# A linear-attention layer with a squared-ReLU feed-forward layer: where the per-token sums are kept, how the weights are laid out and loaded, and the order of the steps

## The chip, the cores and the metric

The kernel runs on one core of one Trainium2 chip. The metric is device time in microseconds (us) of one execution, the median of several runs. The engines in this text are TensorE (PE: matmuls; PEld: its weight loads), VectorE (DVE), ScalarE (ACT), GpSimd (POOL) and the queue of SyncE (SP), which issues most DMA transfers.

## The reference, cut to what matters

The first stage is a linear attention with a decaying state, for 4 batches and 8 heads of 768 tokens with 48 channels. The second is a feed-forward layer with weights of 384 x 2048 and 2048 x 384.

```python
def _attn_ref(r, k, v, w, u):
    state = zeros((B, H, D, D))
    for t in range(S):
        cur = einsum('bhd,bhe->bhde', u[None] * kt, vt)
        y[:, :, t] = einsum('bhd,bhde->bhe', rt, state + cur)
        state = w[None, :, :, None] * state + einsum('bhd,bhe->bhde', kt, vt)
    return y
def _moe_ref(x, w_in, w_out):
    r = np.maximum(x @ w_in, 0.0)
    return (r * r) @ w_out
```

All inputs and the output are float32. The output has 3072 x 384 elements.

## The kernel before, in words

The work is cut into 24 units: 6 chunks of 128 tokens, and in each chunk the 4 batches; unit i belongs to chunk i // 4. Each unit goes through these steps, and each step is a small function that emits a few instructions:

- load (L263): r, k and v of the unit, 192 KB each, by SP's queue, in runs of 48 floats.
- scale (L286, DVE): r and k times powers of the decay, to bf16, into one of NPAD padded buffers (rkw). cast_v (L290, ACT) makes vb from v.
- Turning r and k (rkT): for the first NPE = 7 units PE transposes them (turn, L306) and ACT evicts the result (L310); the later units use a DMA transpose on SP's queue (turn_dma, L295).
- at (L323, PE): products of tokens within the chunk, into two PSUM banks; mask (L335, DVE) multiplies them by a triangle and writes am.
- rk (L315, DVE) multiplies the turned r and k; diag (L341, PE) sums it with u for each token and head, into the last 8 columns of the bank of y; diag_v (L349, DVE) makes dv, those sums times v.
- state_mm (L357, PE) forms what the chunk adds to the state, in a bank of its own; state_add, state_decay (L369 to L375, DVE) and state_cast (L381, ACT) bring the state to the next chunk.
- y_mm (L389 and L395, PE): am times vb, and from the second chunk on turned r times the state, added up in the bank of y. Its first matmul does not clear the bank, since diag has begun it. evict_y (L404, DVE) adds dv.
- x: the first NPY = 6 units are turned by PE (L420) and evicted by ACT (L424), the later ones by a DMA transpose (L413).
- mm1 (L436, PE): four steps a unit, each of 12 matmuls with 128 x 128 weights from w_in_sb; relu (L444, ACT), square (L453 on DVE or L451 on ACT, in turn).
- mm2 (L460, PE): four steps a unit of 4 matmuls with 384 columns of w_out; evict_o (L467) and store (L497). The last unit's mm2 is done in two halves (L475, L486, L488, L493).

The weights come by GpSimd's queue (weights, L273 and L277), which also turns float32 into bf16: w_in and w_out each in four pieces of 384 KB (counted in bf16). Ahead of each piece a one-element copy (gate, L269) holds GpSimd until k of a given unit has landed. The order is the list `front` (L523): U is the load of a unit, I and O are the pieces of w_in and w_out, and a piece is gated by the unit named last before it.

The order of everything is planned when the program is built. Plan.run walks through modelled time: each engine takes, of its steps whose inputs are ready and whose buffers or PSUM banks are free, the one with the lowest rank. The step's cost, a lag until its result can be used, and for DMA its queue are given with plan.add (L513 to L658). Ranks are 4 x unit plus an offset: mm1 comes L1 = 9 places and mm2 L2 = 20 places behind the front of its own unit. The engines then execute in this order, each waiting for what it needs. `room` gives the buffers of each kind, and the call of plan.run the banks that each kind may hold of the eight: at 4 (state products among them), y 2, h 4 (mm1's results and turns), o 2.

Of the kernel before, what the change touches and what calls it, by code (L numbers as in the profile page):

```python
# [1 line left out]

# [13 lines left out]
class Plan:  # L16
# [6 lines left out]
    def __init__(self):  # L23
        self.steps = []
        self.at = {}
        self.users = {}
        self.place = {}

    def add(self, key, engine, cost, emit, needs=(), rank=0.0, new=(), uses=(), lag=0.3, move=None):
        s = dict(key=key, engine=engine, cost=cost, emit=emit, rank=rank, new=new, lag=lag, move=move)  # L30
        s["needs"] = [n for n in needs if n is not None]
        self.at[key] = s
        self.steps.append(s)
        for x in tuple(new) + tuple(uses):
            self.users.setdefault(x, []).append(s)

    def run(self, room, banks, count):
# [15 lines left out]
        def done(s):  # L53
            return "ready" in s and s["ready"] <= t + tiny

        def fits(s):
            names = [x[0] for x in s["new"]]
            for name in set(names):
                if name in banks:
                    continue  # L60
                ring, m = rings[name], room[name]
                for n in range(len(ring) - m, len(ring) - m + names.count(name)):
                    if n >= 0 and not all(done(x) for x in self.users[ring[n]]):
                        return False
            wanted = [name for name in names if name in banks]
            if wanted:
                for n, x in held.items():
                    if x is not None and all(done(u) for u in self.users[x]):
                        held[n], since[n] = None, max(u["ready"] for u in self.users[x])
                if sum(x is None for x in held.values()) < len(wanted):  # L70
                    return False
                for name in set(wanted):
                    mine = sum(x is not None and x[0] == name for x in held.values())
                    if mine + wanted.count(name) > banks[name]:
                        return False
            return True

        while left:
            for e, mine in todo.items():
                if free[e] > t + tiny:  # L80
                    continue
                for s in mine:
                    if s["move"] and sum(x[1] for x in queues[e]) > 4.0:
                        continue
                    if all(done(self.at[k]) for k in s["needs"]) and fits(s):
# [11 lines left out]
                        if s["move"]:  # L97
                            queues[e].append([s, s["move"][0], free[e] + 0.9])
                        else:
                            s["ready"] = free[e] + s["lag"]  # L100
# [6 lines left out]
            later += [s["ready"] for s in order[-400:] if s.get("ready", 0.0) > t + tiny]  # L107
# [8 lines left out]
            for x in moving:  # L116
                x[1] -= step * x[0]["move"][1] / whole
                if x[1] <= 1e-7:
                    queues[x[0]["engine"]].pop(0)
                    x[0]["ready"] = t + x[0]["lag"]  # L120
# [4 lines left out]
def kernel(  # L125
# [21 lines left out]
    NPE = 7  # L147
    NPY = 6
    NPAD = 4
    SQUARES = 'MA'  # L150
# [4 lines left out]
    loads = ctx.enter_context(tc.tile_pool(name="loads", bufs=5))  # L155
# [3 lines left out]
    mpool = ctx.enter_context(tc.tile_pool(name="mpool", bufs=5))  # L159
    psum = ctx.enter_context(tc.tile_pool(name="psum", bufs=1, space=PSUM))  # L160
    banks = [psum.tile([128, 512], F32, name=f"bank{n}") for n in range(8)]
    plan = Plan()
# [105 lines left out]
    def weights(i, q, which):  # L268
        nc.gpsimd.tensor_copy(gate, tiles[i]["kt"][:, 0, :1])  # L269
        if which == "I":  # L270
            sl = slice(q * dff // NQ, (q + 1) * dff // NQ)
            src = moe_w_in.rearrange("(ko ki) f -> ki ko f", ki=128)
            nc.gpsimd.dma_start(out=w_in_sb[:, :, sl], in_=src[:, :, sl])  # L273
        else:
            sl = slice(q * NF // NQ, (q + 1) * NF // NQ)
            src = moe_w_out.rearrange("(ko ki) f -> ki ko f", ki=128)
            nc.gpsimd.dma_start(out=w_out_sb[:, sl, :], in_=src[:, sl, :])  # L277
# [59 lines left out]
    def diag(i):  # L337
        t = tiles[i]
        t["y"] = bank("y", i)[:, : dm + H]
        for p in range(HP):  # L340
            nc.tensor.matmul(  # L341
                out=t["y"][:, dm:], lhsT=t["rk"][:, p, :], rhs=uwb[:, p, :],
                start=(p == 0), stop=(p == HP - 1), skip_group_check=True,
            )

    def diag_v(i):
        t = tiles[i]
        t["dv"] = work.tile([C, H, D], F32, name="dv")
        nc.vector.tensor_tensor(  # L349
            t["dv"], t["vb"], t["y"][:, dm:].unsqueeze(2).to_broadcast([C, H, D]), ALU.mult  # L350
        )

    def state_mm(i):
        t = tiles[i]
        t["s"] = bank("at", i, 2)[:, :dm].rearrange("p (a d) -> p a d", a=HP)
        for p in range(HP):
            nc.tensor.matmul(  # L357
                out=t["s"][:, p, :], lhsT=t["rkw"][:, 1, p].rearrange("p o e -> p (o e)"),
                rhs=t["vb"][:, 2 * p : 2 * p + 2, :].rearrange("p h d -> p (h d)"),
                start=True, stop=True, skip_group_check=True,  # L360
            )
# [21 lines left out]
    def y_mm(i):  # L383
        c, b = units[i]
        t = tiles[i]
        y = t["y"][:, :dm].rearrange("p (h d) -> p h d", h=H)
        for o in range(2):
            for p in range(HP):
                nc.tensor.matmul(  # L389
                    out=y[:, 2 * p + o, :], lhsT=t[f"am{o}"][:, p, :], rhs=t["vb"][:, 2 * p + o, :],  # L390
                    start=False, stop=c == 0 and o == 1 and p == HP - 1, skip_group_check=True,
# [9 lines left out]
    def evict_y(i):  # L401
        t = tiles[i]
        t["yb"] = work.tile([C, dm], BF16, name="yb")
        nc.vector.tensor_tensor(t["yb"], t["y"][:, :dm], t["dv"].rearrange("p h d -> p (h d)"), ALU.add)  # L404
# [21 lines left out]
    def mm1(i, m, s):  # L426
# [5 lines left out]
        for a in range(4 // m):  # L432
            f = s * (4 // m) + a
            for n in range(NK):
                turned = w_in_sb[:, n, f * 128 : (f + 1) * 128]
# [66 lines left out]
    L1, L2 = 9, 20  # L502
# [4 lines left out]
    def add(*a, lag=0.2, **kw):  # L507
        plan.add(*a, lag=lag, **kw)

    def copy(*a, **kw):  # L510
        plan.add(*a, lag=1.2, **kw)

    add("w0", ACT, 3.6, None, rank=-1e3)  # L513
    add("log", PE, 0.64, spread_log, rank=-1e3, needs=["w0"], new=[("h", "log")])
    add("w", ACT, 0.5, do(power, wpos, up), rank=-1e3, needs=["log"], uses=[("h", "log")])
    add("wk", ACT, 0.5, do(power, wneg, down), rank=-1e3, needs=["w"], uses=[("h", "log")])
    copy("begin", SP, 0.74, None, rank=-1e3, move=(0.4, 16))
    copy("wu", SP, 0.9, columns, rank=-99.85, move=(0.1, 16))
# [4 lines left out]
    front = ['U0', 'U1', 'I0', 'U2', 'I1', 'U3', 'I2', 'I3', 'U4', 'O0', 'O1', 'O2', 'O3', 'U5']  # L523
    place = {what: -100 + n for n, what in enumerate(front)}
    seen = -1
    for what in front:
        if what[0] == "U":
            seen = int(what[1:])
        else:
            q = int(what[1])  # L530
            copy(
                (what[0], q), POOL, 1.0, do(weights, seen, q, what[0]), rank=place[what], move=(2.05, 74),
                needs=[("kt", seen)], uses=[("ld", seen)],
            )
    for i in range(NU):
# [3 lines left out]
        rank = place.get(f"U{i}", a - 20)  # L539
        for n, name in enumerate(("rt", "kt", "vt")):  # L540
            copy(
                (name, i), SP, 0.45, do(load, i, name), rank=rank + 0.1 * n, move=(1.03, 16),
                new=[("ld", i)] if n == 0 else (), uses=[("ld", i)] if n else (),
            )
        for x in range(2):
# [6 lines left out]
            ("vb", i), ACT, 0.405, do(cast_v, i), rank=a + 0.5, needs=[("vt", i), ("rkT", i) if i < 4 else ("scale", i, 1)],  # L552
# [14 lines left out]
        else:  # L567
            copy(("rkT", i), SP, 0.45, do(turn_dma, i), rank=a - 30, needs=both, move=(1.9, 32), new=[("rkT", i)], uses=[("rkw", i)])
# [6 lines left out]
        elif i - 1 in PAIRED:  # L575
            add(("at", i), PE, 0.0, None, rank=a - 3, needs=[("at", i - 1)], lag=0.0)
# [7 lines left out]
        add(("diag", i), PE, 0.105, do(diag, i), rank=a + 2, needs=[("rk", i), "uwb"], new=[("y", i)], uses=[("rk", i)])  # L584
        add(("dv", i), DVE, 0.465, do(diag_v, i), rank=a + 2, needs=[("diag", i), ("vb", i)], new=[("dv", i)], uses=[("y", i), ("vb", i)])
        if c < NCH - 1:
            add(
                ("s", i), PE, 0.17, do(state_mm, i), rank=a + (5 if c else 8), needs=[("scale", i, 1), ("vb", i), ("at", i)],
                new=[("at", i, 2)], uses=[("rkw", i), ("vb", i)],
            )  # L590
            add(
                ("sadd", i), DVE, 0.68, do(state_add, i), rank=a + (6 if c else 3.2),
                needs=[("s", i), ("stb", before) if c else "wend"], uses=[("at", i, 2)],
            )
            if c > 0:
                add(("sdec", i), DVE, 0.27, do(state_decay, i), rank=a + 4 + 4, needs=[("sadd", i)])
            add(
                ("stb", i), ACT, 0.71, do(state_cast, i), rank=a + 6 + 4,
# [4 lines left out]
            needs=[("mask", i, 0), ("mask", i, 1), ("vb", i), ("diag", i), ("stb", before) if c else None],  # L603
            uses=[("am", i, 0), ("am", i, 1), ("vb", i), ("rkT", i), ("y", i)],
# [8 lines left out]
        else:  # L613
            copy(("xT", i), SP, 0.45, do(x_dma, i), rank=a - 30, needs=xneed, move=(0.7, 32), new=xnew, uses=[("yb", i)] + xuse)
    begun = 0
    step = 0
    for m in GROUPS:
# [3 lines left out]
        for s in range(4 * m):  # L621
            rank = 4 * i + s + L1 + 1 * (m - 1)
            add(
                ("m1", i, s), PE, (0, 0.668, 0.655, 0, 0.647)[m], do(mm1, i, m, s), rank=rank,
                needs=[("xT", i + n) for n in range(m)] + [("I", s // m), None if b == 0 and s == 0 else ("m1", i - b, 0)],
# [9 lines left out]
        for j in range(i, i + m):  # L635
            a = 4 * j
            squares = [[("sq", i, s) for s in range(q * m, q * m + m)] for q in range(NQ)]
            if j < NU - 1:
                for q in range(NQ):
                    add(  # L640
                        ("m2", j, q), PE, 0.652, do(mm2, j, q), rank=a + q + L2 + 1 * (m - 1),
# [4 lines left out]
                copy(("out", j), SP, 0.42, do(store, j), rank=a + 4 + L2, needs=[("osb", j)], move=(0.8, 110), uses=[("osb", j)])  # L646
                continue
            for n in range(2):
# [9 lines left out]
                copy(("out", j, n), SP, 0.42, do(store_half, j, n), rank=a + 4 + L2, needs=[("osb", j, n)], move=(0.45, 110), uses=[("osb", j)])  # L658
    room = dict(
        ld=5, rkw=NPAD, g=2, rkT=4, vb=4, rk=4, am=8, dv=4, yb=4, xT=3, gr=5, osb=5,  # L660
    )
    for s in plan.run(room, dict(at=4, y=2, h=4, o=2), len(banks)):
# [32 lines left out]
```

## Time and profile before

| | |
|---|---|
| median of 3 runs | 180.88 us (180.58 to 181.18) |
| the profiled execution | 180.29 us |
| its span, first to last instruction | 178.5 us |
| mean granted TensorE clock | 0.997 |
| busy: PE, DVE, ACT, POOL | 165.4, 136.5, 126.8, 12.0 us |
| DMA: hardware queue q1, software queue q0 | 74.4% and 11.2% of 16 engines' span |

Matmuls are pipelined, so the mean duration of one (223 ns in mm1) is longer than the distance between two starts. Where the cost of a PE step is wanted, the distance from start to start on the timeline, or the piece in the chain of waits, is the number to read. Slices are 178.5 / 40 = 4.46 us wide.

### The profile page before, as it was taken

The page shows a single profiled execution, that of the slowest core. Times are in us where ns is not written, and L with a number is a line of the kernel's source. Part 1 is how long each engine was busy: PE and PEld are TensorE (multiplying, and loading weights), DVE is VectorE, ACT ScalarE, POOL GpSimd, SP SyncE. Part 2 cuts the span into 40 slices and gives each one's busy share as a digit, 9 for nine tenths or more (in the row PEclk, how much of TensorE's full clock was granted, in tenths as well). Part 3 has the DMA queues.
Part 4 walks back from the last instruction along what each step waited for, and adds up shares of the span by engine and source line. Part 5 has one row for each costly group of instructions (what it writes and reads, how often), then busy time and mean ns, then how long its engine had stood idle before and what let it go on. Part 6 is the DMA issues. An engine that isn't in the chain of part 4 may idle for free. (4 is left out here: it accounts for less than half of the span.)

```text
span 178.5 us, 5489 instructions
## 1 busy us (share of the span) xinstructions
PE 165.4 (93%) x2270; PEld 132.4 (74%) x2270; DVE 136.5 (76%) x291; ACT 126.8 (71%) x256; POOL 12.0 (7%) x38
## 2 busy tenths in 40 slices
PE   2487889999999999999999999999999999999993
PEld 1366889877786868877868787787787788787872
DVE  4498799854997999979979969988988967573300
ACT  4546399998968466977848985976875875597811
POOL 3451253000000000000000000000000000000000
PEclk9999999999999999999999999999999999999998
DMA  4999999999989998998969998799878976414112
GB/s 89 192 179 219 176 214 201 185 188 193 165 164 113 192 167 175 150 222 178 185 114 225 132 209 177 167 156 218 185 140 196 190 163 199 121 24 70 44 44 88
DMA packets 107682, 28.60 MB, mean 160 GB/s; under 512 B 100873, under 2 KB 107658, under 8 KB 107658
## 3 DMA queue, kind: packets, MB, share of 16 engines
q1 hardware_dynamic: 103944, 25.11, 74.4%
q0 software_dynamic: 3712, 3.15, 11.2%
q8 instruction: 17, 0.28, 0.7%
q14 instruction: 7, 0.06, 0.1%
q10 hardware_dynamic: 2, 0.00, 0.0%
HBM read 20.45 MB, written 4.72 MB: 141 GB/s over the span
## 5 line engine op out<-in xcount | busy, mean ns | idle before, releaser
L436 PE MATMUL bank<-xT,w_in_sb 128*128 128x128 bf16 x1152 | 77.1, 223 | 0.6 <-ACT xT L424 0.6
L436 PEld LDWEIGHTS <-w_in_sb 128*128 128x128 bf16 x1152 | 69.4, 100 | 5.1 <-issue 0.7
L444 ACT ACTIVATE gr<-bank 128x512 f32<-128x512 f32 x96 | 55.0, 596 | 24.2 <-PE bank L436 21.8
L460 PE MATMUL bank<-w_out_sb,g 128*128 128x384 bf16 x368 | 67.5, 326 | 0.0
L460 PEld LDWEIGHTS <-g 128*128 128x128 bf16 x368 | 33.5, 98 | 17.8
L453 DVE TENSOR_TENSOR g<-gr 128x512 bf16<-128x512 f32 x48 | 32.9, 687 | 16.6 <-ACT gr L444 16.3
L335 DVE TENSOR_TENSOR am<-bank,smask 128x512 bf16<-128x512 f32 x48 | 31.1, 685 | 6.3 <-PE bank L323 6.0
L451 ACT ACTIVATE g<-gr 128x512 bf16<-128x512 f32 x48 | 30.3, 634 | 0.9
L467 ACT COPY osb<-bank 128x384 f32<-128x384 f32 x23 | 11.0, 477 | 9.3 <-PE bank L460 9.1
L381 ACT CAST stb<-st 64x192 bf16<-64x192 f32 x40 | 13.9, 347 | 3.8 <-DVE st L375 3.4
L286 DVE TENSOR_TENSOR rkw<-rt,wpos 128x384 bf16<-128x384 f32 x24 | 13.3, 552 | 3.7 <-ACT wpos L238 2.6
L404 DVE TENSOR_TENSOR yb<-bank,dv 128x384 bf16<-128x384 f32 x24 | 13.3, 555 | 2.8 <-PE bank L389 1.7
L349 DVE TENSOR_TENSOR dv<-vb,bank 128x384 f32<-128x384 bf16 x24 | 13.1, 546 | 0.5 <-PE bank L395 0.2
L286 DVE TENSOR_TENSOR rkw<-kt,wneg 128x384 bf16<-128x384 f32 x24 | 13.2, 550 | 0.0
L290 ACT CAST vb<-vt 128x384 bf16<-128x384 f32 x24 | 12.3, 511 | 0.1
L323 PE MATMUL bank<-rkT 64*128 64x128 bf16 x192 | 10.2, 229 | 1.8 <-ACT rkT L310 1.8
L371 DVE TENSOR_TENSOR st<-bank,st 64x192 f32<-64x192 f32 x32 | 11.3, 352 | 0.2
L315 DVE TENSOR_TENSOR rk<-rkT 128x512 bf16<-128x512 bf16 x24 | 10.1, 420 | 1.6 <-ACT rkT L310 1.4
L310 ACT COPY rkT<-bank 128x512 bf16<-128x512 bf16 x14 | 8.2, 587 | 4.3 <-PE bank L306 4.0
L389 PEld LDWEIGHTS <-am 128*128 128x128 bf16 x192 | 8.3, 99 | 3.9 <-issue 2.7
L389 PE MATMUL bank<-vb,am 128*128 128x48 bf16 x192 | 9.1, 187 | 1.7 <-DVE dv L349 1.6
L323 PEld LDWEIGHTS <-rkT 64*128 64x128 bf16 x192 | 5.8, 98 | 5.7 <-ACT rkT L310 2.3
(52 smaller groups left out, 88.1 us busy)
## 6 DMA issues: line engine op xcount, KB each, us to landing
rt<-in_r_dram SPq DMA_DIRECT2D x24, 192.0 KB, 4.4
kt<-in_k_dram SPq DMA_DIRECT2D x24, 192.0 KB, 4.0
vt<-in_v_dram SPq DMA_DIRECT2D x24, 192.0 KB, 4.2
out_dram<-osb SPq DMA_DIRECT2D x23, 192.0 KB, 3.1
w_in_sb<-in_moe_w_in_dram POOLq DMA_DIRECT2D x4, 384.0 KB, 6.1
w_out_sb<-in_moe_w_out_dram POOLq DMA_DIRECT2D x4, 384.0 KB, 8.7
xT<-yb SPq DMA_TRANSPOSE x18, 3.5
rkT<-rkw SPq DMA_TRANSPOSE x17, 3.6
```

The lines of the kernel that those rows point to most:

```text
L286: nc.vector.tensor_tensor(t["rkw"][:, x, :, :, :D], pair(src), pair(wx), ALU.mult)
L323: nc.tensor.matmul(out=t["at"][o][:, p, :], lhsT=t["rkT"][sl, 1, p, :], rhs=t["rkT"][sl, 0, p, :], start=True, stop=True,)
L335: nc.vector.tensor_tensor(am, t["at"][o], smask.unsqueeze(1).to_broadcast([C, HP, C]), ALU.mult)
L349: nc.vector.tensor_tensor(t["dv"], t["vb"], t["y"][:, dm:].unsqueeze(2).to_broadcast([C, H, D]), ALU.mult)
L381: nc.scalar.copy(stb[b][sl, :, o * D : (o + 1) * D], st32[b][sl])
L389: nc.tensor.matmul(out=y[:, 2 * p + o, :], lhsT=t[f"am{o}"][:, p, :], rhs=t["vb"][:, 2 * p + o, :], start=False, stop=c == 0 and o == 1 an ...
L404: nc.vector.tensor_tensor(t["yb"], t["y"][:, :dm], t["dv"].rearrange("p h d -> p (h d)"), ALU.add)
L436: nc.tensor.matmul(out=t["h", s][:, a], lhsT=turned, rhs=chunks[c]["xT"][:, n, b : b + m, :], start=(n == 0), stop=(n == NK - 1),)
L444: nc.scalar.activation(t["gr", s], t["h", s], AF.Relu)
L451: nc.scalar.activation(g, x, AF.Square)
L453: nc.vector.tensor_tensor(g, x, x, ALU.mult)
L460: nc.tensor.matmul(out=t["o"], lhsT=chunks[units[i][0]]["g"][:, f, units[i][1], :], rhs=w_out_sb[:, f, :], start=(f == 0), stop=(f == NF - 1),
```

## The change

The diff is one of many small pieces; they fall into six groups.

- Sums in the state's bank: diag and state_mm become one step, sums, which writes the state products and the diagonal sums into one bank (kind s). y_mm gets a bank that it begins itself, and it no longer needs diag. In the last chunk only the diagonal sums are formed.
- w_in is loaded in two pieces instead of four. w_out is still loaded in four, but a partition gets four adjacent rows of a quarter of it. So that the hidden units match, mm1 takes for each block of 128 hidden units every fourth column of w_in (a step of four elements in the weight operand).
- NPE goes from 7 to 5 and NPY from 6 to 4: units 5 and 6 (r and k) and 4 and 5 (x) are turned by DMA instead of PE. NPAD goes from 4 to 5.
- More buffers: loads 5 to 7, relu results and output tiles 5 to 8, banks of kind h 4 to 5. Squares begin on ACT instead of DVE.
- The order: other ranks (L1 from 9 to 7, loads from 20 to 12 places ahead, DMA transposes from 30 to 10, state steps earlier), another `front` list, and the loads of w and u on SP between the first r and the first k instead of after the first k. vb of the first four units waits for the scaled k, no longer for rkT.
- The planner: the time until a result can be used depends on the engines at both ends (five numbers given to Plan), and DMA steps carry their own queue limits and delays.

The core of the diff:

```diff
-    NPE = 7
-    NPY = 6
-    NPAD = 4
-    SQUARES = 'MA'
+    NPE = 5
+    NPY = 4
+    NPAD = 5
+    SQUARES = 'AM'
...
-    plan = Plan()
+    plan = Plan((0.9, 0.0, 0.1, 0.4, 0.12))
...
         if which == "I":
-            sl = slice(q * dff // NQ, (q + 1) * dff // NQ)
+            sl = slice(q * dff // NQ, (q + 2) * dff // NQ)
...
-            src = moe_w_out.rearrange("(ko ki) f -> ki ko f", ki=128)
-            nc.gpsimd.dma_start(out=w_out_sb[:, sl, :], in_=src[:, sl, :])
+            src = moe_w_out.rearrange("(q ki a) d -> ki q a d", q=NQ, a=NF // NQ)
+            nc.gpsimd.dma_start(out=w_out_sb[:, sl, :], in_=src[:, q])
...
+    def sums(i):
+        c, b = units[i]
+        t = tiles[i]
+        t["s"] = bank("s", i)[:, :dm].rearrange("p (a d) -> p a d", a=HP)
+        t["d"] = bank("s", i)[:, dm : dm + H]
         for p in range(HP):
             nc.tensor.matmul(
+                out=t["d"], lhsT=t["rk"][:, p, :], rhs=uwb[:, p, :],
+                start=(p == 0), stop=(p == HP - 1 and c == NCH - 1), skip_group_check=True,
+            )
+        for p in range(HP if c < NCH - 1 else 0):
             nc.tensor.matmul(
                 out=t["s"][:, p, :], lhsT=t["rkw"][:, 1, p].rearrange("p o e -> p (o e)"),
                 rhs=t["vb"][:, 2 * p : 2 * p + 2, :].rearrange("p h d -> p (h d)"),
-                start=True, stop=True, skip_group_check=True,
-            )
+                start=False, stop=(p == HP - 1), skip_group_check=True,
+            )
...
-        y = t["y"][:, :dm].rearrange("p (h d) -> p h d", h=H)
+        t["y"] = bank("y", i)[:, :dm]
+        y = t["y"].rearrange("p (h d) -> p h d", h=H)
...
-                    start=False, stop=c == 0 and o == 1 and p == HP - 1, skip_group_check=True,
+                    start=(o == 0 and p == 0), stop=c == 0 and o == 1 and p == HP - 1, skip_group_check=True,
...
-                turned = w_in_sb[:, n, f * 128 : (f + 1) * 128]
+                turned = w_in_sb[:, n, :].rearrange("p (q f a) -> p q a f", q=NQ, a=NF // NQ)[:, f // 4, f % 4, :]
...
-    L1, L2 = 9, 20
+    L1, L2 = 7, 20
...
-    copy("wu", SP, 0.9, columns, rank=-99.85, move=(0.1, 16))
+    copy("wu", SP, 1.46, columns, rank=-99.95, move=(0.1, 16, 0.67, 0.1))
...
-    front = ['U0', 'U1', 'I0', 'U2', 'I1', 'U3', 'I2', 'I3', 'U4', 'O0', 'O1', 'O2', 'O3', 'U5']
+    front = ['U0', 'U1', 'I0', 'U2', 'I2', 'U3', 'O0', 'O1', 'O2', 'U4', 'O3', 'U5']
...
-        rank = place.get(f"U{i}", a - 20)
+        rank = place.get(f"U{i}", a - 12)
...
-            copy(("rkT", i), SP, 0.45, do(turn_dma, i), rank=a - 30, needs=both, move=(1.9, 32), new=[("rkT", i)], uses=[("rkw", i)])
+            copy(("rkT", i), SP, 1.24, do(turn_dma, i), rank=a - 10, needs=both, move=(1.5, 26, 0.67, 1.0), new=[("rkT", i)], uses=[("rkw", i)])
...
-        ld=5, rkw=NPAD, g=2, rkT=4, vb=4, rk=4, am=8, dv=4, yb=4, xT=3, gr=5, osb=5,
+        ld=7, rkw=NPAD, g=2, rkT=4, vb=4, rk=4, am=8, dv=4, yb=4, xT=3, gr=8, osb=8,
     )
-    for s in plan.run(room, dict(at=4, y=2, h=4, o=2), len(banks)):
+    for s in plan.run(room, dict(at=4, s=2, y=2, h=5, o=2), len(banks)):
```

## The prediction

> **What bounds the kernel now.** I read the page first: busy shares and the row of slices, then the chain that ended last, then the timeline of TensorE (PE), and last GpSimd's and the DMA queues in the first 40 us.
>
> ```profile
> span 178.5 us, 5489 instructions
> PE 165.4 (93%) x2270; PEld 132.4 (74%) x2270; DVE 136.5 (76%) x291; ACT 126.8 (71%) x256; POOL 12.0 (7%) x38
> PE   2487889999999999999999999999999999999993
> DMA  4999999999989998998969998799878976414112
> L436 PE MATMUL bank<-xT,w_in_sb 128*128 128x128 bf16 x1152 | 77.1, 223 | 0.6 <-ACT xT L424 0.6
> ```
>
> PE has 9 tenths from the seventh slice (about 27 us) to the last but one; only the first six show room. So PE's order sets the end, and time is won where PE idles, runs slowly, or has less to do. The chain from 100 us to 175.5 us is PE nearly throughout. Its pieces (start, duration, what) give the price of a step:
>
> ```profile
> 100.29 0.47 DVE dv L349
> 100.77 0.04 issue
> 100.81 0.36 PE bank L389 x8
> 101.17 0.17 PE bank L395 x4
> 101.34 0.17 PE bank L357 x4
> 101.51 2.60 PE bank L460 x16
> 104.11 1.34 PE bank L436 x24
> ...
> 107.50 0.20 PE bank L389 x8
> ```
>
> 24 matmuls of mm1 take 1.34 us, 56 ns each with their weight load; 8 of y_mm take 0.20 us, 25 ns each with theirs. And at 100.29 PE waits for VectorE's (DVE) dv, since y_mm writes the bank from which dv reads the diagonal sums. After 25 us the waits view puts 1.2 us in 5 waits on this pair.
>
> The start is different. TensorE's timeline shows 12 matmuls of mm1 from 16.99 to 18.27 us, 107 ns each: half the later pace, though the granted clock reads full. The pace turns at about 24 us. Up to 25 us PE waits 7.9 us: 3.1 for the first logarithm, 2.5 for turns of r and k (scaling, and the eviction before them), 1.3 for rkT ahead of the decay products, 0.6 for xT, 0.4 on dv. It never waits for w_in. GpSimd's rows show when weights are asked for:
>
> ```profile
> 9.40 0.92 POOL L273 DMA_DIRECT2D w_in_sb<-in_moe_w_in_dram  x1
> 12.01 0.18 POOL L269 COPY gate<-kt 128x1 f32<-128x1 f32 x1 [1.69 <-DMA kt<-in_k_dram]
> 12.46 0.79 POOL L273 DMA_DIRECT2D w_in_sb<-in_moe_w_in_dram  x1 [0.28 <-issue]
> 17.05 0.18 POOL L269 COPY gate<-kt 128x1 f32<-128x1 f32 x1 [3.80 <-DMA kt<-in_k_dram]
> ...
> 18.39 0.78 POOL L273 DMA_DIRECT2D w_in_sb<-in_moe_w_in_dram  x1
> 24.18 0.39 POOL L269 COPY gate<-kt 128x1 f32<-128x1 f32 x1 [5.01 <-DMA kt<-in_k_dram]
> ```
>
> A quarter of w_in lands 5.8 to 8.7 us after its issue, a quarter of w_out 6.5 to 11.5. The DMA engines are full until some 150 us, so bytes early in the queue decide who starts when.
>
> **The change, part by part.**
>
> Fewer PE transposes. NPE goes 7 to 5, NPY 6 to 4: four half-turns of r and k (units 5 and 6) and two x turns (units 4 and 5) leave PE. On the timeline a half-turn starts at 38.53 and the next step at 38.75 (0.22); an x turn at 35.05, the next step at 35.22 (0.17). 4 x 0.22 + 2 x 0.17 = 1.22 us, all after 22 us where PE is dense. One half-turn also came late (m2 from 45.16 takes 0.65, the turn begins at 46.10): 0.29 us more. ScalarE (ACT) loses 4 x 0.59 + 2 x 0.48 us, which is off the path. In exchange SP's queue gets two more transposes of rkT (1.25 us of issue each, 3.6 to landing) and two of xT (1.20 and 3.5). The loads behind them wait some 4.9 us of queue time in all. That lies beside a backlog: mm1 and mm2 of older units follow the front by L1 and L2 places. Uncovered it would cost one stall of 3.6. In DMA time, q1 takes 94.1% of 50 to 110 us; at some 9.4 units (PE's 6.4 us a unit) that is 6.0 us a unit. A unit's three loads are 3,072 of these packets, at 18.3 ns over 16 engines 3.5 us (8,723 packets in 1.5 to 11 us, 104.8%). So transposes and store are at most 2.5, and two units add at most 5. The DMA row falls to 1 to 7 tenths after 150 us, so I cost it at nothing. Together: -1.5 us, ends -1.5 and +3.6.
>
> Sums in the state's bank. The diagonal sums move from y's bank to that of the state's products; y_mm then no longer waits for dv. The matmuls are the same. The waits view gives 1.6 us in six waits over the run, and the timeline's gaps ahead of the six late y_mm after 25 us, less a normal step, come to about 2.2. What is late next is the second mask, which DVE ends 0.47 us before dv ends; only the 0.6 us gap at 100 us is longer than that. The new wait: the diagonal matmuls now also wait for vb and the scaled k, and PE's queue stands behind them. dv needed vb before too, and PE's waits name vb for only 0.3 us. I take -1.6; ends 0 and -2.2.
>
> Strided weights. Each mm1 weight load reads every fourth column. No row of before reads weights with a step. Packed loads fit into 25 ns with their matmul (y_mm above); mm1's pace is 56. So a strided load may take 2.2 times a packed one at no cost, and above that each ns costs 1,152 ns. The load's own recorded duration, 100 ns, is the upper end: (100 - 56) x 1,152 = 51 us. Below nothing is excluded, as the matmul's own 128 columns set the 56. I take 0, nearest to the 25 ns row, and keep 51 as a rival. [...]
>
> Weights in other pieces. A packet of w_in (2 KB read) takes 99.6 ns (803 in 11 to 19 us at 62.5% of 16 engines), one of w_out (1.5 KB) 76.7 (2,076 in 27.5 to 39 us at 86.5%). The line through both has 8 ns that don't grow with the size, so 4 KB and 6 KB runs save about 8 x 768 + 8 x 1,536 ns over 16 engines, 1.2 us of DMA time: an estimate from two contended windows, hidden behind PE's backlog.
>
> The order at the start. The first w_in piece is twice as large. Issued at 9.4, with 0.9 of issue and some 1.1 to the first byte, its 9.6/2 us of transfer at full or at 62.5% share lands it at 16.2 to 19.1, against a first mm1 at 16.99: up to 2.1 late. But with it two steps of each ready unit can run instead of one. The second half waits for kt of unit 2 (12.01) and not of unit 3 (17.05), and w_out for kt of unit 3 and not of unit 4 (24.18), seven us earlier, queued behind w_in: w_out's first quarter comes some 4 us sooner. The load of unit 4 shares the engines with w_out; by then mm1 of four units (16 x 0.67) and mm2 (4 x 2.6) are in stock. On SP, the two small w and u loads move ahead of the first kt, which then is issued 1.4 us later; its scaling ends at 6.54 and PE's turn of it starts at 7.33 only after an eviction, so 0.8 of that is covered. By 25 us PE has done four mm1 steps; I expect one or two more (0.67 each). I take -1.0, ends +2.5 (late half, late kt) and -4 (dense from 18 us on).
>
> Larger buffers, ranks and the planner's lags change the order everywhere. After 25 us PE's waits beyond dv come to 0.5 us, so there is little to win; I cost them at 0, ends -0.5 and +2. The end (last half store, 175.5 to 178.5) stays.
>
> **Sum.** -1.5 - 1.6 - 1.0 = -4.1. The profiled execution took 180.29 (span 178.5 and 1.8 around it): 176.2 on that scale. The median is 0.6 higher: 176.8.
>
> **Rivals.**
> 1. Strided weights are slower than mm1's pace. For: no row shows them, and weight loads record 100 ns. [...] It decides from 56 + 4.1/1.152 = 59.6 ns a load; at 100 it gives 176.8 + 51 = 228. Slower. Chance 0.10.
> 2. The start turns round: the larger first half comes after mm1 is due and the later unit 4 or 5 and its DMA transpose leave PE idle, which then stays at the 107 ns pace. For: DMA full, every early wait is on a tile's data. Price: +2.5 for the start instead of -1.0, +3.6 for one uncovered transpose: 176.8 + 7.1 = 184 at the end, 181.5 to 184 in the main. Chance 0.13.
> 3. The start opens: PE dense and at full pace from 18 us on, -4 instead of -1: 173.8, with all of the y_mm gaps 173.2. Chance 0.12.
> 4. Nothing gained at the start and masks late in dv's place: only the turns count, 179.4; about 0.08 that it ends between 178.8 and 180.3, and 0.07 that it lies within 0.3%.
> The forecast, 174.5 to 178.8, has 0.50.
>
> **Numbers.** About 0.3% (0.54 us) is what a measurement of this kernel can tell from no change. Faster 0.50 + 0.12 + 0.08 = 0.70, same 0.07, slower 0.10 + 0.13 = 0.23. The range leaves out rival 1 and the outer ends of 2 and 3: 173.3 to 183.0.
>
> **What would show it.** Turns: L306 x40 and L420 x12, 19 and 20 DMA transposes. Sums: no wait of y_mm on dv. Strided: 24 mm1 matmuls in the chain still 1.34 us; 1.5 or more proves rival 1. Start: mm1's matmuls reach 56 ns before 24 us, and PE's slices two to six rise; a wait of mm1 on the w_in load speaks for rival 2. I am wrong if PE gets new gaps after 40 us: then the order, which no row of before shows, is what counts.

## The result, and the profile after

The changed kernel takes 188.12 us (median, 187.92 to 188.76) against 181.03 for the kernel before on the same chip: 1.045 times as long (95% interval 1.039 to 1.050; the quotient of the two medians, 1.039, is its lower end). The forecast was 176.8, with 173.3 to 183.0 as the range. The profiled execution took 188.1 us with a span of 186.3. In what follows a ratio is always to the kernel before on the same chip. Some kernels below have scattered executions: the ratios leave disturbed ones out, the medians and the profiles of e1, e5 and e14 do not, so where the two disagree the ratio is the one to compare.

From the page of the changed kernel: the span, the rows of PE and DMA, and mm1's two groups (now L458). Against the page of before, PE's fifth slice (18.6 to 23.3 us) is empty, and 7s and 8s stand in the middle; the DMA row has a hole of 0 and 3 at 37 to 47 us.

```profile
span 186.3 us, 5404 instructions
PE   3484099999999999999799998999989999979992
DMA  3999999903998797869989969999998997892011
L458 PE MATMUL bank<-xT,w_in_sb 128*128 128x128 bf16 x1152 | 73.5, 222 | 7.8 <-DMA w_in_sb<-in_moe_w_in_dram 5.6
L458 PEld LDWEIGHTS <-w_in_sb 128*128 128x128 bf16 x1152 | 69.0, 115 | 10.8 <-DMA w_in_sb<-in_moe_w_in_dram 6.1
```

PE's timeline shows the hole: one matmul of mm1 runs, and the next waits 5.12 us for a load of w_in.

```profile
17.54 0.29 PE L458 MATMUL bank<-xT,w_in_sb 128*128 128x128 bf16 x1 [0.52 <-DMA w_in_sb<-in_moe_w_in_dram]
22.95 4.75 PE L458 MATMUL bank<-xT,w_in_sb 128*128 128x128 bf16 x47 [5.12 <-DMA w_in_sb<-in_moe_w_in_dram]
```

On the timeline of the weight loads (PEld) the first one of mm1 waits for w_in until 17.53 us, as it must. The second one waits until 22.94, when the second half has landed (in the chain of waits its transfer lasts from 12.70 to 22.90), though the columns that it reads lie in the first half. In the kernel before, no such wait is there.

```profile
17.53 0.11 PEld L458 LDWEIGHTS <-w_in_sb 128*128 128x128 bf16 x1 [0.79 <-DMA w_in_sb<-in_moe_w_in_dram]
22.94 1.20 PEld L458 LDWEIGHTS <-w_in_sb 128*128 128x128 bf16 x12 [5.30 <-DMA w_in_sb<-in_moe_w_in_dram]
```

The chain of waits has 24 matmuls of mm1 in the same 1.34 us as before. So the strided weights don't slow mm1 down, and no line of the page has y_mm waiting for dv any more.

```profile
39.44 1.34 PE bank L458 x24
```

SP's timeline shows the hole in the DMA row: after a load of v at 26.49 (7.08 us to issue) the queue stands until the x transpose of unit 4 can go at 42.96, and the loads of the next units stand behind it. Only a part of this comes from the late start: in e1 below, which has no such wait, the queue still stands from 32.1 to 37.9 us.

```profile
26.49 7.08 SPq L288 DMA_DIRECT2D vt<-in_v_dram  x1
42.96 1.30 SPq L435 DMA_TRANSPOSE xT<-yb  x1
44.31 0.57 SPq L288 DMA_DIRECT2D rt<-in_r_dram  x1
```

After 50 us PE waits 3.4 us on DMA transposes. The first two rows are all of its waits on them there (us in total, times, longest); the third is the kernel before, where y_mm's wait for dv is PE's only one after 50 us:

```profile
PE bank L458 <- DMA xT<-yb: 2.1, 3, 1.2
PE bank L348 <- DMA rkT<-rkw: 1.3, 2, 1.1
PE bank L389 <- DVE dv L349: 0.9, 4, 0.4
```

### The profile page after: what moved, and what is told of

The parts are those of the page before. It is cut to its first block, busy times and chain, and to the rows that moved or that the text cites. A ratio compares the mean times of both kernels' runs of the same rounds, so it can differ in the third digit from the quotient of the medians.

```text
span 186.3 us, 5404 instructions
## 1 busy us (share of the span) xinstructions
PE 164.2 (88%) x2248; PEld 129.9 (70%) x2248; DVE 136.9 (73%) x293; ACT 122.1 (66%) x250; POOL 10.4 (6%) x34
## 4 chain that ended last, share of the span: by engine, by line
PE 53%; DMA 28%; DVE 7%; ACT 5%; SPq 3%; issue 1%; POOL 0%; DVEq 0%; ACTq 0%; POOLq 0%
PE bank L482 22%; PE bank L458 22%; DMA rkT<-rkw 9%; DMA xT<-yb 7%; DMA w_in_sb<-in_moe_w_in_dram 5%; DMA kt<-in_k_dram 4%; DMA rt<-in_r_dram 3%; SPq L288 2%; PE bank L348 2%; ACT gr L466 2%; DVE yb L426 1%; PE bank L411 1%; PE bank L497 1%; ACT g L473 1%; DVE am L360 1%
## 5 line engine op out<-in xcount | busy, mean ns | idle before, releaser
L458 PE MATMUL bank<-xT,w_in_sb 128*128 128x128 bf16 x1152 | 73.5, 222 | 7.8 <-DMA w_in_sb<-in_moe_w_in_dram 5.6
L458 PEld LDWEIGHTS <-w_in_sb 128*128 128x128 bf16 x1152 | 69.0, 115 | 10.8 <-DMA w_in_sb<-in_moe_w_in_dram 6.1
L466 ACT ACTIVATE gr<-bank 128x512 f32<-128x512 f32 x96 | 53.2, 593 | 22.9 <-PE bank L458 22.7
L335 ACT COPY rkT<-bank 128x512 bf16<-128x512 bf16 x10 | 5.9, 585 | 4.2 <-PE bank L331 4.1
```

The lines of the kernel that those rows point to most:

```text
L458: nc.tensor.matmul(out=t["h", s][:, a], lhsT=turned, rhs=chunks[c]["xT"][:, n, b : b + m, :], start=(n == 0), stop=(n == NK - 1),)
L466: nc.scalar.activation(t["gr", s], t["h", s], AF.Relu)
```

## Experiments

Three theories at first: A, the wait for the second half; B, the larger packets of the halves starve the loads; C, the new order. All 18 runs:

| run | what | median us | ratio to before (95%) |
|---|---|---|---|
| changed kernel | | 188.1 | 1.045 (1.039 to 1.050) |
| e1 | changed, w_in in two tiles | 183.0 | 1.016 (1.006 to 1.027) |
| e2 | changed, old layout | 184.1 | 1.022 (1.013 to 1.032) |
| e3 | before, new layout | 196.4 | 1.094 (1.084 to 1.105) |
| e4 | before, new layout, four tiles | 181.0 | 1.004 (1.000 to 1.008) |
| e5 | e1, NPE 7 and NPY 6 | 184.7 | none; 180.8 to 185.3 |
| e6 | changed, four tiles, quarters | 184.4 | 1.021 (1.012 to 1.031) |
| e7 | e1, old ranks | 184.2 | 1.023 (1.014 to 1.032) |
| e8 | before, sums alone | 177.4 | 0.985 (0.976 to 0.994) |
| e9 | e1, old planner | 189.7 | 1.051 (1.046 to 1.055) |
| e10 | e8, new planner | 184.2 | 1.010 (1.003 to 1.017) |
| e11 | e8, new layout, four tiles | 177.2 | 0.981 (0.976 to 0.987) |
| e12 | e8, NPE 5 and NPY 4 | 182.4 | 1.008 (1.003 to 1.013) |
| e13 | e10, limit 4.0 | 183.4 | 1.020 (1.009 to 1.032) |
| e14 | e1, limit 4.0 | 188.1 | 1.036 (1.020 to 1.052) |
| e15 | e1, 20 stores left out | 179.0 | 0.996 (0.992 to 1.001) |
| e16 | e5, limit 4.0 | 184.1 | 1.027 (1.015 to 1.038) |
| e17 | e10, transposes planned 2.2 us earlier | 179.2 | 0.995 (0.991 to 1.000) |
| e18 | e1, transposes planned 2.2 us earlier | 184.8 | 1.026 (1.019 to 1.033) |

### The wait for the other half: e1 to e4

e1:

```diff
-    w_in_sb = const.tile([128, NK, dff], BF16)
+    w_in_sb = [const.tile([128, NK, dff // 2], BF16, name=f"w_in_sb{n}") for n in range(2)]
...
-turned = w_in_sb[:, n, :].rearrange("p (q f a) -> p q a f", q=NQ, a=NF // NQ)[:, f // 4, f % 4, :]
+turned = w_in_sb[f // 8][:, n, :].rearrange("p (q f a) -> p q a f", q=2, a=NF // NQ)[:, f // 4 % 2, f % 4, :]
```

> The changed kernel, with w_in in two tiles, one for each half; nothing else differs. Theory A (a wait that was not needed): in the changed kernel the first strided weight load waits for the first half of w_in, but the second one waits for the second half too, though it reads only the first; PE stands still for 5.1 us (17.8 to 22.95), SP's queue then stands for 10.2 us in front of the x transpose of unit 4, the DMA engines idle from 37.5 to 43 us, and the later waits for loads and DMA transposes are the echo of that. By A the 12 first matmuls of mm1 run together from about 17.5 us and the time falls by 5 us or more: 180 to 183.5. Theory B (big packets): a 4 KB packet of w_in takes its turn at the engines against a 192-byte packet of a load, so the loads starve while w_in comes in; kt of unit 3 still lands at about 24 us, and the time falls by less than 2 us: above 186. Theory C (order): the new ranks and the four added DMA transposes make the PE gaps after 40 us by themselves: about 6 us of gaps after 40 us stay, 183 to 186.

e2 (mm1 and w_out take the old two lines again):

```diff
-turned = w_in_sb[:, n, :].rearrange("p (q f a) -> p q a f", q=NQ, a=NF // NQ)[:, f // 4, f % 4, :]
+turned = w_in_sb[:, n, f * 128 : (f + 1) * 128]
```

> The changed kernel with the old layout of the weights alone: packed columns of w_in as weights, w_out rows as before (1.5 KB runs); w_in still in two halves and the new order. Theory A: the wait for the second half goes as with two tiles, the same time as that run within 0.7 us. Theory B: w_in's 4 KB packets stay and w_out's fall to a quarter; within 1 us of the changed kernel, 187 to 189. If strided weight loads cost PE time by themselves, it is faster than the run with two tiles by more than 1 us, and mm1's matmuls are closer than there.

e3 (the same two places of the kernel before, the other way round):

```diff
-turned = w_in_sb[:, n, f * 128 : (f + 1) * 128]
+turned = w_in_sb[:, n, :].rearrange("p (q f a) -> p q a f", q=NQ, a=NF // NQ)[:, f // 4, f % 4, :]
```

> The kernel before with the new layout alone (strided columns as weights, w_out as four adjacent rows), w_in still in four quarters in one tile. Theory A: the second weight load waits for the second quarter also, a later one for the third and fourth; PE stands 1 to 2 us at about 17 us, and the time grows by 0.5 to 3 us: 181.4 to 184. Theories B and C: no change from the wait, 180.4 to 181.6.

e4 (as e3, but a tile for each quarter):

```diff
+    w_in_sb = [const.tile([128, NK, dff // NQ], BF16, name=f"w_in_sb{n}") for n in range(NQ)]
+turned = w_in_sb[f // 4][:, n, :].rearrange("p (f a) -> p a f", a=NF // NQ)[:, f % 4, :]
```

> The kernel before with the new layout as in the run above, but w_in in four tiles, one for each quarter, so that no load of weights can wait for a quarter that it does not read. Theory A: within 0.6 us of the kernel before, 180.4 to 181.6, and below the run above. If the strided load costs PE time, mm1's distance from start to start is above 56 ns and the time grows by 1.15 us for each ns. Theory B: w_out's packets of 6 KB read hold up the loads of units 4 and 5 in 27 to 39 us; slower by 0.5 to 2 us.

With two tiles the wait is gone. PE's timeline of e1 has the 48 first matmuls of mm1 in one piece from 17.72 us, 5.2 us earlier, and the ratio falls from 1.045 to 1.016, some 5 us:

```profile
17.72 4.74 PE L458 MATMUL bank<-xT,w_in_sb 128*128 128x128 bf16 x48 [0.70 <-DMA w_in_sb<-in_moe_w_in_dram]
```

One part of theory A failed: the later waits on DMA transposes are no echo of this wait. The profile of e1, taken of its longest execution (185.05 us), has 6.3 us of them after 50 us, and e2, which hasn't this wait either, 4.2 us in all.

e3 puts the layout alone into the kernel before, and it costs 9.4% (some 16 us), five times the most that theory A expected (3 us). GpSimd's timeline of e3 shows why: the wait also goes the other way. The third and the fourth load of w_in wait for mm1, which by then reads only the first ones, as if its reads and these loads overlapped, and PE then waits 12.0 us for w_in in all:

```profile
24.94 0.78 POOL L273 DMA_DIRECT2D w_in_sb<-in_moe_w_in_dram  x1 [7.64 <-PE bank L436]
...
32.81 0.78 POOL L273 DMA_DIRECT2D w_in_sb<-in_moe_w_in_dram  x1 [6.90 <-PE bank L436]
```

e4 is the same layout with a tile for each quarter: 0.4% above the kernel before, with an interval of 0.0 to 0.8%. So the layout costs nothing that can be told from no change, and the wait for a piece that isn't read is shown. That e2 (packed, no such wait) and e1 (strided) agree within their intervals says the same of the weight loads. How the framework decides on overlap is not shown; that it takes the whole stretch between a stepped slice's or a load's first and last element would give what is seen.

### What else the change costs: e5 to e8

> The changed kernel with w_in in two tiles, and units 5 and 6 (r and k) and 4 and 5 (x) turned by PE again (NPE 7, NPY 6). Theory C1 (the added DMA transposes): with two tiles SP's queue stood from 32.1 to 37.9 us in front of the x transpose of unit 4, with all later loads behind it, the DMA engines ran at 3 tenths there, and PE then waits 6.3 us on DMA transposes and gaps of 0.7 to 1.8 us come at 57, 84, 115, 132 and 161 us. With the turns on PE the queue doesn't stand there: those waits fall to less than 2.5 us, and the time goes from 183.0 to 180.5 to 182, although PE has 1.2 us more to do. Theory C2 (ranks): the waits on DMA transposes stay at 4 us or more, 182.5 to 184.5.

```diff
-    NPE = 5
-    NPY = 4
+    NPE = 7
+    NPY = 6
```

> The changed kernel with w_in in four tiles and four loads, in the order that the kernel before has (second quarter after unit 2, third and fourth after unit 3, w_out after unit 4). Theory B (the halves starve the loads): kt of unit 3 lands at about 17 us instead of 24, and the time falls below that with two tiles (183.0) by 1 us or more. If B is not it, 182 to 184, with the waits on DMA transposes as they were (about 6 us).

```diff
-front = ['U0', 'U1', 'I0', 'U2', 'I2', 'U3', 'O0', 'O1', 'O2', 'U4', 'O3', 'U5']
+front = ['U0', 'U1', 'I0', 'U2', 'I1', 'U3', 'I2', 'I3', 'U4', 'O0', 'O1', 'O2', 'O3', 'U5']
```

> The changed kernel with w_in in two tiles, and the old places of the loads (20 ahead), of the DMA transposes (30 ahead) and of mm1 (L1 9). Theory C2 (ranks: loads too late): PE's waits on DMA transposes fall below 3 us and the time to 180.5 to 182. Theory C1: SP's queue still stands in front of the x transpose of unit 4, 182.5 to 184.5.

```diff
-    L1, L2 = 7, 20
+    L1, L2 = 9, 20
...
-        rank = place.get(f"U{i}", a - 12)
+        rank = place.get(f"U{i}", a - 20)
```

(and rkT and xT at a - 30.)

> The kernel before with the sums in the state's bank alone (its own ranks for the state's steps, layout and loads as before). As predicted for this step: y_mm no longer waits for dv, and the time falls by 1.6 us, between 0 and 2.2: 178.4 to 180.6. Rival: the diagonal sums now wait for vb, and the time stays within 0.5 us or grows.

```diff
-    for s in plan.run(room, dict(at=4, y=2, h=4, o=2), len(banks)):
+    for s in plan.run(room, dict(at=4, s=2, y=2, h=4, o=2), len(banks)):
```

(with sums, diag_v, y_mm and their steps as in the change, and the old ranks of the state's steps.)

e5 is inconclusive: one execution took 180.8 us and three about 185. e6 and e7 miss: in e6 k of unit 3 passes GpSimd's gate at 16.94 us instead of 24.05 in e1, just as B wants, and the time does not fall. So B is real in the queues, but e6 as a whole gains nothing; in exchange its w_out is asked for at 26.95 instead of 24.52 us, and PE waits 1.5 us for it. The ranks alone (e7) are not it either.

e8 is a hit in sign and mechanism: the sums alone gain 1.5%, and the median, 177.4, lies a little below the expected range. The waits view of e8 from 50 us on has no row at all for PE; in the kernel before, y_mm waited there for dv.

### The parts of the order, one at a time: e9 to e12

> The changed kernel with w_in in two tiles and the old planner (its lags and its limit of 4 us of transfers outstanding on SP's queue), all ranks, costs, buffers and transposes as changed. So far two tiles gave 183.0, and none of undoing the transposes, the halves or the ranks alone went below 182 reliably, while the kernel before with the sums alone gave 177.4: 5.6 us lie in the order. Theory C3 (the planner's rules): the new planner lets SP's queue run later and puts a DMA transpose ahead of loads that could go; with the old rules loads go earlier, PE's waits on DMA transposes and data fall below 2.5 us and the time to 177.5 to 180. Rival C4 (the ranks and the added DMA transposes): no change, 182 to 185.

(edit: the class Plan and the lags 0.2 and 1.2 of the kernel before, in e1.)

> The kernel before with the sums in the state's bank and the new planner with its costs, lags and limits, but the old ranks, transposes, buffers, layout and loads. C3: it loses what lies between, 177.4 becomes 180 to 184, with waits of PE on DMA transposes. C4: within 1 us of 177.4.

(edit: the class Plan and the costs, lags and move figures of the change, in e8.)

> The kernel before with the sums in the state's bank and the new layout (strided columns as weights, four adjacent rows of w_out), w_in in four tiles so that no weight load waits for a quarter that it does not read. If the layout costs nothing by itself, as with the sums left alone: within 0.8 us of 177.4, 176.6 to 178.2.

(edit: e4's two lines and w_out's layout, in e8.)

> The kernel before with the sums in the state's bank and NPE 5, NPY 4: four half-turns and two x turns go from PE to DMA transposes. As predicted for this step: -1.2 to -1.5 us, 175.9 to 176.2; C1 and C4 (SP's queue stands in front of a transpose, the loads behind it come late): 178.5 to 182, with waits of PE on DMA transposes and xT.

```diff
-    NPE = 7
-    NPY = 6
+    NPE = 5
+    NPY = 4
```

e11, sums and new layout, beats both kernels: 0.981 of before, which its interval doesn't tell from the sums alone (e8, 0.985). e9 contradicts C3, that the new planner's rules are what costs in the changed kernel: the old planner with the other changes is slower still, 1.051. But e10 and e12 each put one part into the kernel with sums, and each turns 0.985 into more than 1: the new planner +2.5% (by two of e10's four executions, 181.8 and 183.7 us; the others took 184.7 and 184.9), the four half-turns and two x turns by DMA +2.3%.

In e12 the place can be pointed at. The x transpose of unit 4 takes 5.63 us to issue instead of 1.2, in front of later loads. PE then waits for a mask, for a transpose and for rk between 53 and 57 us, 3.2 us in three waits. That the late loads cause these waits is read from the order of the queue; no run separates it. The windows from 54 us on (start and end, length, busy time of PE, PEld, DVE, ACT, POOL, granted clock, DMA share, GB/s; e12, e12, and e8 for comparison) show the rest: with PE busy 3.20 of 6 us, the granted clock drops to 0.69 and 0.74 for two windows, where e8 has 1.00.

```profile
33.58 5.63 SPq L410 DMA_TRANSPOSE xT<-yb  x1
```

```profile
53.51 0.27 PE L386 MATMUL bank<-vb,am 128*128 128x48 bf16 x4 [0.33 <-DVE am L335]
54.82 0.40 PE L323 MATMUL bank<-rkT 64*128 64x128 bf16 x8 [0.86 <-DMA rkT<-rkw]
57.20 0.27 PE L343 MATMUL bank<-uwb,rk 128*128 128x8 bf16 x4 [1.99 <-DVE rk L315]
```

```profile
54.00:60.00 6.00, 3.20 (x39) 3.03 (x40) 5.71 (x14) 1.81 (x4) 0.00 (x0) 0.69 0.91 169
60.00:66.00 6.00, 6.00 (x68) 4.86 (x65) 4.33 (x9) 3.63 (x7) 0.00 (x0) 0.74 0.77 157
54.00:60.00 6.00, 6.00 (x98) 4.67 (x96) 4.71 (x11) 3.41 (x8) 0.00 (x0) 1.00 1.08 211
```

In the windows on both sides (48 to 54 and 66 to 72 us) the granted clock of e12 is 1.00. The two low ones together lack 3.4 us of full clock (6.00 x 0.31 + 6.00 x 0.26), as much as the mean clock of 0.981 lacks over the span of 181.0 us: an estimate from these figures. The clock is a part of the cost, not all of it: the two of the eight executions with a mean clock of 0.997 or more took 180.2 and 181.3 us, the five at 0.981 took 182.0 to 182.9, and the eighth, at 0.987, 184.2.

### Lost lead, or transposes too late: e13 to e18

Theory D: the loads lose their lead at the start and never make it up. Loads issued by 48 us were 30 in the kernel before, 22 in the changed one, 25 in e1, 27 in e10 (counted on SP's timeline), and from 48 to 144 us every kernel up to there issues 41 to 43 more.

> The kernel before with sums and the new planner, with the planner's limit on transfers outstanding on SP's queue at 4.0 instead of 1.5; nothing else differs from the run with sums and the new planner (184.2, 27 loads issued by 48 us, 27 loads ahead of the first transpose). Theory D: 30 loads stand ahead of the first transpose again, 29 to 30 are issued by 48 us, and the time falls to 177 to 180. If the order of the steps as such is the cause, 182 to 185.

> The changed kernel with w_in in two tiles and the limit at 4.0 instead of 1.5. Only 20 loads instead of 18 stand ahead of the first x transpose, since that transpose is unit 4's. Theory D: a part of the lead comes back: 26 to 27 loads by 48 us, 181 to 183. If the limit is all, below 180.

> The changed kernel with w_in in two tiles, NPE 7 and NPY 6, and the limit at 4.0: 27 loads and one store stand ahead of the first transpose. Theory D: 28 or more loads by 48 us and 178 to 181. If the other ranks, the halves of w_in or the buffers cost by themselves: 182 or more.

```diff
-for x in queues[e]) > 1.5:
+for x in queues[e]) > 4.0:
```

> The changed kernel with w_in in two tiles, with the stores of the first 20 units left out (those rows of the output are not written); SP's order and all else stay. Theory D: the supply is what PE waits for after 50 us, and 20 stores less give it some 0.6 to 0.8 us a unit back: PE's waits on DMA transposes fall below 3 us and the time to 178 to 181. If the supply doesn't bind, within 1 us of 183.0.

```diff
+        if i >= 20:
             nc.sync.dma_start(out=out[b * S + c * C : b * S + (c + 1) * C, :], in_=tiles[i]["osb"])
```

The lead came back (29 loads by 48 us in e13, 30 in e16; 27 in e14) and the time did not. D falls as the cause. e15 shows that transfers do bind in e1: with 20 stores less, PE's waits on DMA transposes after 50 us go from 6.3 us (in e1's one profile, of 185.05 us) to 1.3 (in one of 179.09), and the ratio from 1.016 to 0.996. Whether the engines or SP's queue is relieved, it cannot tell.

Theory E came from the distance between the issue of a transpose of rkT and the first product that reads it (SP's timeline against PE's, each unit). Its median is 7.6 us in the kernel before, 7.0 in e8, 6.8 in e11, but 4.9 in the changed kernel, 5.0 in e1 and 4.8 in e10. To landing a transpose takes 3.6 to 4.5 us (the medians of these runs) and up to 6.1. So the new planner issues transposes just in time.

> The kernel before with sums and the new planner, whose delay from the end of a DMA transpose to its use is set from 0.9 to 3.1 us; all else as in the run with sums and the new planner (184.2). Theory E (transposes issued just in time): the distance from issue to use rises to about 7 us, PE's waits on DMA transposes fall below 1 us, and the time to 177 to 179.5. If the distance is not it: 182 or more.

> The changed kernel with w_in in two tiles and the same longer delay for rkT and xT. Theory E: the distance rises from 5.0 to about 7 us and the time falls from 183.0 to 178.5 to 181; what stays above 177.2 is SP's stand in front of the transposes of units 4 to 6. If the loads or the order as such bind: 182 to 185.

```diff
-                return s["end"] + moved
+                return s["end"] + (3.1 if s["key"][0] in ("rkT", "xT") else moved)
```

In e17 the distance is 6.6 us, the wait of PE on rkT (2.8 us in e10) is gone, and 1.010 becomes 0.995. So in that kernel E accounts for 1.5 of the 2.5% that the new planner costs; the rest, against e8's 0.985, lies within the intervals. The median distance alone doesn't settle it, though: it is 7.0 us in e13 too, where PE still waits 1.8 us on rkT, in two waits, and the ratio is 1.020. PE's timeline of e10 shows one such wait; the transpose had been issued at 104.18, 6.0 us before:

```profile
110.21 0.40 PE L348 MATMUL bank<-rkT 64*128 64x128 bf16 x8 [0.81 <-DMA rkT<-rkw]
```

In e18 the same edit raises the distance to 6.7 us and removes every wait on DMA transposes after 50 us, and the ratio is 1.026, not below e1's 1.016. PE waits for DVE instead:

```profile
PE bank L368 <- DVE rk L340: 2.0, 2, 1.3
PE bank L482 <- DVE g L475: 1.8, 4, 0.7
PE bank L411 <- DVE am L360: 0.5, 2, 0.3
```

So E is not enough in the changed kernel. What stays open: 3.5% lie between e1 and e11 (1.016 and 0.981). The planner and the turns by DMA each cost about 2.4% by themselves in the kernel with sums, and in the full change taking back one of them, or the ranks, or the quarters, does not bring it down for certain. Both taken back at once was not tried. One caution goes with all of these runs: a changed rank, cost, limit or turn makes the planner write a new order for the whole kernel, so each run tests the part together with the order that came out of it.

## Why the prediction was wrong, point by point

- **Strided weights.** The step priced how fast a stepped weight load is read, and there it was right: 56 ns from start to start, 24 matmuls in 1.34 us, rival 1 (228 us) is out, and the time of e4 agrees with the row of y_mm from which it was argued. It failed in not asking what a stepped slice waits for. "It never waits for w_in" was true of before, and the sum went on as if it held after the change, but for a first half that lands up to 2.1 us late. The wait of 5.12 us and its sequel make up about 5 of the 7 to 8 us by which the changed kernel is slower (1.045 against 1.016 in e1). The recorded load grows from 98 to 113 ns (medians of the kernel before and of the changed one) at that same pace.
- **Sums in the state's bank.** Right: -1.6 predicted, -1.5% or 2.8 us by e8's ratio, with an interval of 1.1 to 4.4 us that holds the 1.6. The waits on dv went, and no mask was late in their place. What e8's other order may have added isn't separated.
- **Fewer PE transposes.** Wrong in sign: -1.5 predicted, +2.3% (4 us) in e12 against e8. The 1.2 us of PE work did go. The cover did not hold: that the 4.9 us which "the loads behind them wait" lie "beside a backlog" was the step that failed. PE stood for 3.2 us between 53 and 57 us, and the fallen clock (0.69 and 0.74 in two windows) added to it. The uncovered price named there (3.6 us) comes near the measured cost, but it was one stall at full clock, so that the sizes agree is partly luck.
- **The order.** "I cost them at 0" failed: the planner alone is +2.5% in e10. The reason given, that PE's waits beyond dv were only 0.5 us, showed that there was little to win, and said nothing of what there was to lose. The distances of 7.6 us (median) at which those waits were small could be read in the trace of before. The sign that the prediction named for this, new gaps of PE after 40 us, came.
- **The start.** -1.0 predicted. In e1, without the false wait, mm1 starts at 17.72 (16.2 to 19.1 was the bound) and runs on, and by 25 us six steps of it are done where one or two more than four were expected, so the start was about as forecast. But w_out's first quarter was not asked for seven us earlier: k of unit 3 passes the gate at 24.00 us, not 17.05, since w_in's 4 KB packets held up its load (in e6, with 2 KB packets, it passes at 16.94). In 12 to 21 us q1 moves 1,329 packets in the changed kernel, 4,254 before. The estimate for the pieces counted only what larger packets save, not what the loads beside them lose. In e6, which has quarters again, the time is no shorter.
- **Rival 2** (the start turns round, 181.5 to 184) named the sign, the place and the row that would show it, a wait of mm1 on w_in, but not the reason: it had the first half come late, and the wait was for the second. It stopped 4 us short.

## What to carry to other kernels

The change of layout changed what each read waits for (in e3 PE waits 12.0 us for w_in, in e4 it has no such wait): before pricing how fast a stepped operand is read, look at what else has been written to its tile, and give each piece that is loaded by itself a tile of its own. In an order written out ahead, the distance from the issue of a transfer to its use is a quantity to read from the trace: waits near zero may mean that it is large enough, not that the transfers are fast (7.6 us before, with 3.6 to landing). And a step taken from the bounding engine and given to a queue can be paid by everything behind it in that queue (in e12 one transpose takes 5.63 us to issue from 33.58 on, and the next load goes out at 39.30): price that before calling it covered.

## What the runs showed of the hardware that was not expected

- In the changed kernel a weight load with a step of four bf16 columns is recorded at 113 ns (median) instead of 98, and mm1's pace stays at 56 ns (24 matmuls in 1.34 us).
- In 12 to 21 us, while 4 KB packets of w_in pass in the changed kernel, the 192-byte packets of the loads get 20.0% of the engines' time (48.7% before, with 2 KB packets).
- In e12 PE has one piece of work between 53.95 and 57.20 us (0.40 us from 54.82), its longest single wait there being 1.99 us. The granted clock is 0.69 in the window of 54 to 60 us and 0.74 in that of 60 to 66 us, though PE is busy throughout the second (6.00 us).
